# Two rounds of attention at a time, an earlier start of the weight fold, and copies that walk in the order of their target

## The chip, the cores and the metric

One core of a Trainium2 chip runs the whole program. The metric is the time of one execution on the device, in microseconds (us). The core's engines run side by side, each through a queue of its own in a fixed order: TensorE (PE, with its weight loads PEld), VectorE (DVE), ScalarE (ACT), GpSimd (POOL), and SyncE (SP), which here only issues DMA transfers. Matmul results land in PSUM, which is cut into banks of 512 float32 per partition; everything else on the chip lives in SBUF.

## The reference

Windowed attention over 4 batches, 8 heads, 576 positions and 64 dimensions; heads 0 to 3 see the last 32 positions ("plain"), heads 4 to 7 see 32 positions with a step of 4 ("dilated"). Two MLPs follow, over 2304 tokens.

```python
scores = scale * np.matmul(q, k.transpose(0, 1, 3, 2))
attn = softmax(np.where(mask, scores, -1e9))      # mask_plain or mask_dil, by head
x = np.matmul(attn, v).transpose(0, 2, 1, 3).reshape(B * S, H * D)   # 2304 x 512
h = x @ w_in ; x = np.maximum(0.01 * h, h) @ w_out                   # 512 -> 2048 -> 512
a = x @ w1 ; b = x @ w2 ; out = ((a * b) @ w3) @ w_out2              # 512 -> 1024 -> 1024 -> 512
```

The weights of the MLPs are float64 in memory. The kernel keeps float32 precision by splitting both operands of a product into a high and a low part and adding three matmuls.

## The kernel before

**MLP 1** runs over seven chunks of tokens, `c` = 0 to 6: 320 and 256 tokens of batch 0 (c 0, 1), the same of batch 1 (c 2, 3), then three chunks of 384 tokens that cover batches 2 and 3. In a chunk, 16 turns `f` of 128 hidden units each: `hidden_steps` makes 12 matmuls into one of two PSUM banks (`ps_h`, `bank`, L95), ACT takes the result out as `g` (L563), DVE and POOL split it into `gs` (L110, L112), and two turns later `project_steps` makes 12 matmuls into `ps_x`. A new `ps_h` has to wait until ACT has taken out the one two turns earlier.

**Attention** is cut into 32 rounds: a pair of heads and 5 or 4 blocks of 64 queries (r = 0 or 1). Rounds 0 to 15 (batches 0, 1) lie in an order written out by hand (`START`, under `manual_schedule`), which also holds the first MLP turns. Rounds 16 to 31 (batches 2, 3) come from the generator `attention` (L511), of which `pace` (L949) advances so many steps in each MLP turn. One round is: `scores` (64-row matmuls into `ps_s`, L394; mask, maximum and exponentials on DVE and ACT), `normalize` (DVE, POOL), `turn_p` (transposes `ps_p`, L451; copies to `pT` on ACT), `value_steps` (64-column matmuls `ps_o`, L472; ACT and DVE write the high and low part of x, L500 and L503). `ps_s`, `ps_p` and `ps_o` share the two banks of `side_bank` (L92). q and k come by `load_qk`, and are turned by PE and copied out of PSUM (`turn_rows`, L374) for batches 0 and 1, turned by DVE (`turn_halves`) for 2 and 3.

**The fold** computes w3 @ w_out2 on the chip, during the chunks c = 4 and 5. It converts 24 float64 blocks (`Convert`: fetch by DMA as `rawf`; POOL and ACT scale, ACT makes two halves as `rf`, DVE joins them as `wf`), splits them (`keep_wo2`, `keep_w3`: ACT and DVE or POOL), stores the 8 blocks of w_out2 to memory and loads them again four times (`load_wo2`), and multiplies (`wp_step`). It begins at `LATE`, turn (4, 13), in `begin_fold`, which first lets attention run out and closes its SBUF pool `att`; the pool `fold` takes that space. `FOLD_PACE` makes 1.35 steps of it in each turn. In the last chunk, c = 6, w1 and w2 are converted in the same way and the product is loaded again and split (`load_wp` into `wpf`, `split_wp` into `wps`, `raww`, `wr` and `w` for the weights). **MLP 2** follows with `gate` (`ps_ab`) and `final` (`ps_y`).

Outside `START` the order on each queue is made at build time by a planner: of what is ready by its own model of durations it takes what stands first in the program. The chip then follows this order on each engine, whatever the real durations are.

Of the kernel before, what the change touches and what calls it, by code (L numbers as in the profile page):

```python
# [8 lines left out]
F32 = mybir.dt.float32  # L9
# [13 lines left out]
DILATION = 4  # L23
# [5 lines left out]
def tile_window_attention_two_mlps(  # L29
# [224 lines left out]
    def load_halves(m, src, o):  # L254


        pi, nm = seq[m // 2], "qk"[m % 2]
        t = att.tile([P, NT, D], F32, tag="nat", name=f"{nm}{pi}", bufs=2)
        for g in range(P // E):
            og = o + g // 2 * S * D + g % 2 * E  # L260
            to = t[g * E : (g + 1) * E]
            x = NT * D - E
            nc.sync.dma_start(
                to.rearrange("p n d -> p (n d)")[:, :x], rows(src, og, [[NT * D, E], [1, x]])
            )
        nat_t[nm, pi] = t

    def turn_halves(m):
        pi, nm = seq[m // 2], "qk"[m % 2]
        t = nat_t.pop((nm, pi))  # L270
        dst = att.tile([P, S], F32, tag=nm + "T", name=f"{nm}T{pi}", bufs=2)
# [85 lines left out]
    def turn_rows(m):  # L357
        pi, nm = seq[m // 2], "qk"[m % 2]
        plain = pair(pi)[2]
        c = 6 if plain else 8  # L360
        n = S // c
        t = nat_t.pop((nm, pi))
        ps = bank2(f"ps_{nm}T{pi}")
        for g in range(2):
            for c1 in range(c // 2):
                src = t[:n, g * (c // 2) + c1].rearrange("p j d -> p (j d)")
                nc.tensor.transpose(ps[:, g, c1 * n : (c1 + 1) * n], src, ident[:n, :n])
        yield
        dst = att.tile([P, S], F32, tag=nm + "T", name=f"{nm}T{pi}", bufs=2)
# [89 lines left out]
    def value_steps(n):  # L459
# [24 lines left out]
        else:  # L484
            spans = []
            for g in range(DILATION):
                j0, j1 = max(0, s0 - g * SR), min(SR, s1 - g * SR)
                if spans and spans[-1][2:] == (j0, j1):
                    spans[-1] = (spans[-1][0], spans[-1][1] + 1, j0, j1)
                elif j0 < j1:  # L490
                    spans.append((g, 1, j0, j1))
# [19 lines left out]
    def attention(n0, n1):  # L511
# [7 lines left out]
        scores(n0)  # L519
        yield  # L520
        scores(n0 + 1)
        normalize(n0)
        yield
        for n in range(n0, n1):
# [12 lines left out]
            run(value_steps(n))  # L537
            m = n // NA * 4
            if n % NA in (2, 3):
                load_v(m + n % NA)  # L540
            elif n % NA in (5, 7):
                load_v(m + 4 + (n % NA == 7))
# [122 lines left out]
    def keep_w3(i):  # L665


        def finish(w, e_hi, e_lo):
# [7 lines left out]
            t = fold.tile([P, 2, 2, NG * P], F32R, tag="w3T", name=f"w3T{i}", bufs=2)  # L676
            split(t[:, 0], t[:, 1], ps.rearrange("p (j r) -> p j r", j=2), e_hi, nc.vector)
            w3T.extend((i // (NI // NG), i % (NI // NG) * 2 + j, t[:, :, j]) for j in range(2))
# [28 lines left out]
    def load_wp(ib):  # L707
        t = late.tile([P, DM], F32, tag="wpf", name=f"wpf{ib}", bufs=1)
# [58 lines left out]
    with ExitStack():  # L767
        make_identity(nc, ident)
        att_es, att = pool("att", "right")
        mask_d = masks = att.tile([P, S // QB, KB], BF16, name="masks")  # L770
        nc.vector.memset(masks, 0.0)
        def build_masks():
# [32 lines left out]
            "K": (rawp, "kr", 2), "W": (woB_p, "woB", NF // 2), "N": (att, "nat", 2), "V": (att, "v", 2)  # L805
# [105 lines left out]
        LATE = (4, 13)  # L911
        FOLD_PACE = 1.35
# [18 lines left out]

        def begin_fold():
            step(*[stream] * 200)
            att_es.close()
            nonlocal fold, fold_es, conv3
            fold_es, fold = pool("fold", "right")
            jobs = [(load_rows, w_out2, jb, keep_wo2(jb)) for jb in range(NI)]
            jobs += [(load_w3, w3, i, keep_w3(i)) for i in range(NI * NI // NG // 2)]

            def fold_tile(tag, dt, bufs):  # L940
                return lambda i: fold.tile([P, 512], dt, tag=tag, name=f"{tag}f{i}", bufs=bufs)

            conv3 = Convert(
                jobs, fold_tile("raw", U64, 2), fold_tile("w", I32, 2), fold_tile("r", I32, 2),
                FOLD_CONV,
            )
            conv3.fetch(2)

        def pace(c):  # L949

            owed[0] += 39 / 28 if c < LATE[0] else 2.25
# [7 lines left out]
        for c, f0, f1 in runs:  # L959
# [4 lines left out]
            if c == NCH - 1:  # L964
                while conv3.made < len(conv3.jobs) or conv3.done or w3T:
                    fold_step()
                fold_es.close()
                first_es, first_y = pool("first", "right")
# [97 lines left out]
```

## Time and profile before

| | us |
|---|---|
| median of 3 runs | 869.25 (868.57 to 869.71) |
| the profiled execution | 868.56 |
| its span, from the first to the last instruction | 866.6 |
| PE busy / PEld busy | 848.2 / 772.0 |
| DVE, ACT, POOL busy | 346.7, 352.6, 210.8 |
| attention of batches 2 and 3 and the MLP turns beside it | about 198 to 362 |
| the fold | about 362 to 495 |
| last chunk of MLP 1 with the conversion of w1 and w2 | about 500 to 568 |

Times in the rows are counted from the first instruction. An engine's busy time is the union of its instructions; matmuls overlap, so the distance between their starts tells PE's pace, and a duration does not. A row's bracket gives the idle time before it and what ended that time. The granted clock is TensorE's, as a share of 2.4 GHz.

### The profile page before, as it was taken

The numbers are of one execution on the slowest core, as the hardware profiler recorded it, in microseconds if no ns is written. First come the engines' busy times: TensorE is split into PE (matmuls) and PEld (weight loads), VectorE is DVE, ScalarE is ACT, GpSimd is POOL, SyncE is SP. The second block draws the span as 40 slices with busy tenths as digits, with TensorE's granted clock in tenths as the row PEclk, the third lists the DMA queues.
The fourth block names the chain that finished last, engine by engine and source line by source line (L and its number), as shares of the span: only waits on it lengthen the run. The fifth ranks groups of instructions, "written<-read, shape, count | busy, mean of one in ns | idle before, by whom it ended". The sixth has DMA issues, their size and how long they took to land.

```text
span 866.6 us, 14693 instructions
## 1 busy us (share of the span) xinstructions
PE 848.2 (98%) x5774; PEld 772.0 (89%) x5774; DVE 346.7 (40%) x704; ACT 352.6 (41%) x879; POOL 210.8 (24%) x236
## 2 busy tenths in 40 slices
PE   7999998999999999999999999999999999999998
PEld 7799997999999999989899999998888888888887
DVE  4999976344453432274434177731021011000000
ACT  4999945223443343364433175632131121111111
POOL 3311101122322232263222134223123112111110
PEclk9999999999999999999999999999999999999999
DMA  6976575183333311189887575341001000000001
GB/s 152 309 214 231 179 169 137 34 193 73 82 98 92 78 45 50 47 294 349 300 289 236 165 239 155 113 135 49 25 1 61 24 13 13 25 12 13 25 13 48
DMA packets 87333, 103.58 MB, mean 120 GB/s; under 512 B 42849, under 2 KB 65633, under 8 KB 87265
## 3 DMA queue, kind: packets, MB, share of 16 engines
q1 hardware_dynamic: 87264, 102.65, 39.0%
q8 instruction: 45, 0.74, 0.4%
q14 instruction: 24, 0.19, 0.1%
HBM read 85.72 MB, written 16.91 MB: 118 GB/s over the span
## 4 chain that ended last, share of the span: by engine, by line
PE 77%; DMA 7%; DVE 6%; ACT 5%; issue 4%; POOL 2%; SPq 0%; POOLq 0%; DVEq 0%; ACTq 0%
PE ps_ab L120 7%; PE ps_ab L122 7%; PE ps_ab L121 7%; PE ps_x L120 6%; PE ps_x L122 5%; PE ps_x L121 5%; PE ps_h L120 5%; PE ps_h L122 5%; PE ps_h L121 5%; PE ps_y L122 4%; PE ps_y L121 4%; PE ps_y L120 4%; PE ps_s L394 2%; PE ps_o L472 2%; PE ps_wp L122 2%
## 5 line engine op out<-in xcount | busy, mean ns | idle before, releaser
L120 PE MATMUL ps_h<-x,win 128*128 128x384 f32 (+2 forms) x448 | 142.5, 318 | 4.9 <-ACT g L563 4.2
L122 PE MATMUL ps_h<-x,win 128*128 128x384 f32 (+2 forms) x448 | 140.7, 314 | 0.0
L121 PE MATMUL ps_h<-x,win 128*128 128x384 f32 (+2 forms) x448 | 140.4, 313 | 0.0
L120 PE MATMUL ps_x<-gs,wout 128*128 128x384 f32 (+2 forms) x368 | 119.0, 325 | 0.0
L743 DVE TENSOR_TENSOR ab<-a,ps_ab 128x512 f32<-128x512 f32 (+1 forms) x40 | 25.2, 633 | 233.3 <-ACT a L741 225.8
L120 PE MATMUL ps_ab<-ys,w 128*128 128x512 f32 (+1 forms) x320 | 117.7, 368 | 0.6 <-DVE ab L743 0.6
L121 PE MATMUL ps_x<-gs,wout 128*128 128x384 f32 (+2 forms) x368 | 117.7, 320 | 0.1
L122 PE MATMUL ps_ab<-ys,w 128*128 128x512 f32 (+1 forms) x320 | 117.7, 368 | 0.0
L121 PE MATMUL ps_ab<-ys,w 128*128 128x512 f32 (+1 forms) x320 | 117.6, 368 | 0.0
L122 PE MATMUL ps_x<-gs,wout 128*128 128x384 f32 (+2 forms) x368 | 117.4, 319 | 0.0
L112 POOL TENSOR_TENSOR p<-ab,p 128x512 fp32r<-128x512 f32 (+1 forms) x40 | 47.0, 1177 | 211.3 <-ACT p L110 211.3
L110 DVE CAST gs<-g 128x384 fp32r<-128x384 f32 (+2 forms) x92 | 41.3, 449 | 128.9 <-ACT g L563 103.3
L120 PEld LDWEIGHTS ps_h<-x,win 128*128 128x128 f32 x448 | 84.8, 189 | 8.2 <-ACT g L563 6.1
L112 POOL TENSOR_TENSOR gs<-g,gs 128x384 fp32r<-128x384 f32 (+2 forms) x64 | 59.5, 929 | 133.5 <-DVE gs L110 133.5
L563 ACT ACTIVATE g<-ps_h 128x384 f32<-128x384 f32 (+2 forms) x112 | 49.1, 439 | 96.8 <-PE ps_h L122 80.2
L121 PEld LDWEIGHTS ps_h<-x,win 128*128 128x128 f32 x448 | 84.9, 190 | 0.3
L122 PEld LDWEIGHTS ps_h<-x,win 128*128 128x128 f32 x448 | 84.8, 189 | 0.4
L741 ACT COPY a<-ps_ab 128x512 f32<-128x512 f32 (+1 forms) x40 | 21.6, 543 | 139.5 <-PE ps_ab L122 139.5
L120 PEld LDWEIGHTS ps_x<-gs,wout 128*128 128x128 f32 x368 | 69.5, 189 | 1.7
L121 PEld LDWEIGHTS ps_x<-gs,wout 128*128 128x128 f32 x368 | 69.7, 189 | 1.3 <-POOL gs L112 0.4
L122 PEld LDWEIGHTS ps_x<-gs,wout 128*128 128x128 f32 x368 | 69.7, 189 | 0.6
L120 PEld LDWEIGHTS ps_ab<-ys,w 128*128 128x128 f32 x320 | 60.1, 188 | 11.1 <-DVE ab L743 1.0
(109 smaller groups left out, 1553.1 us busy)
## 6 DMA issues: line engine op xcount, KB each, us to landing
wo<-wo_dram SPq DMA_DIRECT2D x32, 512.0 KB
raw<-in_moe_w_in_dram SPq DMA_DIRECT2D x16, 512.0 KB
raw<-in_moe_w_out_dram SPq DMA_DIRECT2D x16, 512.0 KB
rawf<-in_moe_w_dram SPq DMA_DIRECT2D x16, 512.0 KB
raww<-in_moe_w_dram SPq DMA_DIRECT2D x16, 512.0 KB
q<-in_q_dram SPq DMA_DIRECT2D x48, 140.0 KB
k<-in_k_dram SPq DMA_DIRECT2D x48, 140.0 KB
v<-in_v_dram SPq DMA_DIRECT2D x60, 96.0 KB
```

The costliest lines, as they stand in the source:

```text
L110: copy_on(e_hi)(hi, src)
L112: e_lo.tensor_tensor(lo, src, hi.bitcast(F32), op=ALU.subtract)
L120: nc.tensor.matmul(ps, a[1], b[0], start=first, stop=False)
L121: nc.tensor.matmul(ps, a[0], b[1], start=False, stop=False)
L122: nc.tensor.matmul(ps, a[0], b[0], start=False, stop=last)
L394: nc.tensor.matmul(ps[j * QB : (j + 1) * QB, i - bl.start], qt[d, i * QB : (i + 1) * QB], kt[d, first_key(i, plain) : first_key(i, plain) ...
L472: nc.tensor.matmul(ps[j * D : (j + 1) * D, i * QB : (i + 1) * QB], vt[i][:, h + j, :], t[:, i, j * QB : (j + 1) * QB], start=True, stop=True,)
L563: nc.scalar.activation(g, ps, AF.Prelu, alpha=SLOPE)
L741: nc.scalar.copy(t, ps[0][:, :n])
L743: nc.vector.tensor_tensor(g, t, ps[1][:, :n], op=ALU.mult)
```

## The change

It does five things.

1. **Two rounds at a time**: `attention` steps through rounds n and n + 1 together, in four steps instead of eight: transposes of n; transposes of n + 1 with the turning and loading of q and k; values of both; scores and normalization of the next two. `pace` takes 22/28 and 14/13 steps a turn instead of 39/28 and 2.25. Where the next batch begins (n % 8 == 4), turning and loading come after the scores.
2. **An own pool for q and k**: `nat`, `qT` and `kT` move from `att` to a new pool `qkp`, which stays open until the last chunk.
3. **Earlier fold**: at turn (4, 10) `begin_conv` makes the fold's `Convert` with its buffers in the slots of `nat`, `qT` and `kT`, and fetches two blocks; at (4, 13) one conversion step comes ahead of `begin_fold`.
4. **Buffers**: the transposed blocks of w3 are kept as two halves with 3 buffers, instead of whole with 2, and are split half by half; `wpf` has 2 buffers instead of 1.
5. **Order of copies**: the copies of q and k out of PSUM and the dilated copies of x go through their elements in the order in which these lie in the target.

```diff
-        t = att.tile([P, NT, D], F32, tag="nat", name=f"{nm}{pi}", bufs=2)
+        t = qkp.tile([P, NT, D], F32, tag="nat", name=f"{nm}{pi}", bufs=2)
...
         if plain:
-            to = dst.rearrange("d (p g c) -> d g c p", g=2, p=n)
+            to, dims = dst.rearrange("d (p g c) -> d p g c", g=2, p=n), "d g (c p) -> d p g c"
         else:
-            to = dst.rearrange("d (c p g) -> d g c p", g=2, p=n)
-        copy_on(engine_of[TURN_ON[m]])(to, ps[:, :, : S // 2].rearrange("d g (c p) -> d g c p", p=n))
+            to, dims = dst.rearrange("d (c p g) -> d c p g", g=2, p=n), "d g (c p) -> d c p g"
+        copy_on(engine_of[TURN_ON[m]])(to, ps[:, :, : S // 2].rearrange(dims, p=n))
...
-            x = x.rearrange("d i (j r) -> d i r j", r=DILATION)
-            for g, m, j0, j1 in spans:
+            x = x.rearrange("d i (j r) -> d i j r", r=DILATION)
+            edges = sorted({0, s0 % SR, s1 % SR, SR})
+            for j0, j1 in zip(edges, edges[1:]):
+                g = [g for g in range(DILATION) if s0 <= g * SR + j0 and g * SR + j1 <= s1]
                 src = bass.AP(
-                    ps.tensor, ps.offset + g * SR + j0 - s0,
-                    [list(ps.ap[0]), [SR, m], [1, j1 - j0]],
+                    ps.tensor, ps.offset + g[0] * SR + j0 - s0,
+                    [list(ps.ap[0]), [1, j1 - j0], [SR, len(g)]],
                 )
-                views.append((x[:, :, g : g + m, j0:j1], src))
+                views.append((x[:, :, j0:j1, g[0] : g[-1] + 1], src))
...
+        for n in range(n0, n1, 2):
             run(turn_p(n))
-            normalize(n + 1)
             yield
-            if n % 8 != 3:
-                scores(n + 2)
-                yield
-            transpose_qk(n + 4)
-            load_qk(n + 6)
+            run(turn_p(n + 1))
+            turn = [lambda m=m: (transpose_qk(m), load_qk(m + 2)) for m in (n + 4, n + 5)]
+            if n % NA != 4:
+                for f in turn:
+                    f()
             yield
-            if n % 8 == 3:
-                scores(n + 2)
-                yield
-            run(value_steps(n))
+            for i in (n, n + 1):
+                run(value_steps(i))
...
+            yield
+            for i in (n + 2, n + 3):
+                scores(i)
+            if n % NA == 4:
+                for f in turn:
+                    f()
+            for i in (n + 2, n + 3):
+                normalize(i)
             yield
...
-            t = fold.tile([P, 2, 2, NG * P], F32R, tag="w3T", name=f"w3T{i}", bufs=2)
-            split(t[:, 0], t[:, 1], ps.rearrange("p (j r) -> p j r", j=2), e_hi, nc.vector)
+            for j in range(2):
+                t = fold.tile([P, 2, NG * P], F32R, tag="w3T", name=f"w3T{i}_{j}", bufs=3)
+                split(t[:, 0], t[:, 1], ps[:, j * NG * P : (j + 1) * NG * P], e_hi, nc.vector)
...
-        t = late.tile([P, DM], F32, tag="wpf", name=f"wpf{ib}", bufs=1)
+        t = late.tile([P, DM], F32, tag="wpf", name=f"wpf{ib}", bufs=2)
...
+        CONV_AT = (4, 10)
...
+        def begin_conv():
+            nonlocal conv3
+            jobs = [(load_rows, w_out2, jb, keep_wo2(jb)) for jb in range(NI)]
+            jobs += [(load_w3, w3, i, keep_w3(i)) for i in range(NI * NI // NG // 2)]
+
+            def words(tag, dt):
+                return lambda i: qkp.tile([P, 512], dt, tag=tag, name=f"{tag}f{i}", bufs=2)
+
+            conv3 = Convert(jobs, words("nat", U64), words("qT", I32), words("kT", I32), FOLD_CONV)
+            conv3.fetch(2)
...
-            owed[0] += 39 / 28 if c < LATE[0] else 2.25
+            owed[0] += 22 / 28 if c < LATE[0] else 14 / 13
...
+                if (c, f) == CONV_AT:
+                    begin_conv()
                 if (c, f) == LATE:
+                    conv3.step()
                     begin_fold()
```

## Rows read from the trace of the kernel before

**Rows 1.** The page's first part: busy time, share of the span, instructions.

```profile
PE 848.2 (98%) x5774; PEld 772.0 (89%) x5774; DVE 346.7 (40%) x704; ACT 352.6 (41%) x879; POOL 210.8 (24%) x236
```

**Rows 2.** Stretches: length, busy PE, PEld, DVE, ACT, POOL, clock, DMA share, GB/s.

```profile
345.00:361.80 16.80, 16.80 (x122) 15.81 (x121) 1.93 (x5) 3.49 (x9) 3.05 (x3) 1.00 0.01 3
...
385.40:388.70 3.30, 3.30 (x12) 3.30 (x11) 3.16 (x4) 1.56 (x3) 2.76 (x3) 0.50 0.98 315
388.80:400.00 11.20, 11.07 (x66) 10.69 (x65) 4.38 (x8) 6.62 (x11) 5.50 (x6) 1.00 1.00 369
198.00:362.00 164.00, 164.00 (x1522) 154.62 (x1521) 61.61 (x155) 62.88 (x241) 45.28 (x52) 1.00 0.28 69
```

**Rows 3.** PE in order of time: start, duration; two rounds' values at once.

```profile
156.50 0.28 PE L121 MATMUL ps_x<-gs,wout 128*128 128x256 f32 x1
156.62 0.28 PE L122 MATMUL ps_x<-gs,wout 128*128 128x256 f32 x1
156.83 1.39 PE L472 MATMUL ps_o<-pT,v 96*64 96x64 f32 x40
...
158.37 0.28 PE L121 MATMUL ps_x<-gs,wout 128*128 128x256 f32 x1
```

**Rows 4.** PE in order of time: one round's values.

```profile
269.67 0.28 PE L122 MATMUL ps_h<-x,win 128*128 128x256 f32 x1
269.88 0.69 PE L472 MATMUL ps_o<-pT,v 96*64 96x64 f32 x16
...
270.71 0.28 PE L121 MATMUL ps_x<-gs,wout 128*128 128x256 f32 x1
```

**Rows 5.** PE in order of time: two rounds' scores at once.

```profile
177.50 0.31 PE L122 MATMUL ps_x<-gs,wout 128*128 128x320 f32 x1
177.74 1.54 PE L394 MATMUL ps_s<-kT,qT 64*64 64x96 f32 x32
...
179.46 0.31 PE L121 MATMUL ps_x<-gs,wout 128*128 128x320 f32 x1
```

**Rows 6.** PE in order of time: one round's scores.

```profile
246.42 0.28 PE L121 MATMUL ps_h<-x,win 128*128 128x256 f32 x1
246.63 0.88 PE L394 MATMUL ps_s<-kT,qT 64*64 64x96 f32 x16
...
247.66 0.28 PE L120 MATMUL ps_x<-gs,wout 128*128 128x256 f32 x1
```

**Rows 7.** PE: the first and the last of the small-matmul runs between 198 and 362.

```profile
198.43 0.34 PE L472 MATMUL ps_o<-pT,v 96*64 96x64 f32 x4
...
359.31 0.34 PE L472 MATMUL ps_o<-pT,v 96*64 96x64 f32 x4
```

**Rows 8.** PE and ACT in order of time, where the fold begins.

```profile
381.70 0.34 PE L121 MATMUL ps_h<-x,win 128*128 128x384 f32 x1
381.87 0.34 PE L122 MATMUL ps_h<-x,win 128*128 128x384 f32 x1
384.26 0.45 PE L120 MATMUL ps_h<-x,win 128*128 128x384 f32 x1 [2.05 <-ACT g L563]
...
361.89 0.78 ACT L151 ACTIVATE rf<-rawf 128x512 f16<-128x512 f32 x1
...
381.96 0.62 ACT L110 CAST wo<-wf 128x512 fp32r<-128x512 f32 x1 [2.70 <-DVE wf L157]
```

**Rows 9.** PE and ACT in order of time, in the last chunk of MLP 1.

```profile
545.86 0.44 PE L120 MATMUL ps_h<-x,win 128*128 128x384 f32 x1 [0.65 <-ACT g L563]
...
544.80 0.62 ACT L110 CAST wps<-wpf 128x512 fp32r<-128x512 f32 x1 [0.24 <-DMA wpf<-wp_dram]
```

**Rows 10.** Copies out of PSUM: minimum, median, maximum ns; by shape: busy, mean ns.

```profile
L374 DVE COPY kT<-ps_kT x3: 760/1184/1202, 8.9 to 25.8; 128x576 f32<-128x576 f32 x3
...
L500 ACT CAST x<-ps_o 128x288 fp32r<-128x288 f32 x8 | 5.4, 676 | 9.2 <-PE ps_o L472 9.2
...
L500 ACT CAST x<-ps_o 128x320 fp32r<-128x320 f32 x8 | 3.4, 419 | 2.0 <-PE ps_o L472 2.0
```

More of the change, by code (lines that the diff above doesn't have):

```diff
@@ L270, in turn_halves @@
         t = nat_t.pop((nm, pi))
-        dst = att.tile([P, S], F32, tag=nm + "T", name=f"{nm}T{pi}", bufs=2)
+        dst = qkp.tile([P, S], F32, tag=nm + "T", name=f"{nm}T{pi}", bufs=2)
         if pair(pi)[2]:
@@ L368, in turn_rows @@
         yield
[L369 removed]
+        dst = qkp.tile([P, S], F32, tag=nm + "T", name=f"{nm}T{pi}", bufs=2)
         if plain:
[L371 removed]
+            to, dims = dst.rearrange("d (p g c) -> d p g c", g=2, p=n), "d g (c p) -> d p g c"
         else:
[L373 to L374 removed]
+            to, dims = dst.rearrange("d (c p g) -> d c p g", g=2, p=n), "d g (c p) -> d c p g"
+        copy_on(engine_of[TURN_ON[m]])(to, ps[:, :, : S // 2].rearrange(dims, p=n))
         qk_t[nm, pi] = dst
@@ L518, in attention @@
         load_v(n0 // 2 + 1)
-        scores(n0)
+        for n in (n0, n0 + 1):
+            scores(n)
         yield
-        scores(n0 + 1)
-        normalize(n0)
+        for n in (n0, n0 + 1):
+            normalize(n)
         yield
-        for n in range(n0, n1):
+        for n in range(n0, n1, 2):
             run(turn_p(n))
-            normalize(n + 1)
             yield
-            if n % 8 != 3:
-                scores(n + 2)
-                yield
-            transpose_qk(n + 4)
-            load_qk(n + 6)
+            run(turn_p(n + 1))
[3 more added lines that the diff above has]
+                    f()
             yield
-            if n % 8 == 3:
-                scores(n + 2)
-                yield
-            run(value_steps(n))
+            for i in (n, n + 1):
+                run(value_steps(i))
             m = n // NA * 4
[L539 to L542, printed above, removed]
+            if n % NA == 2:
+                load_v(m + 2)
+                load_v(m + 3)
+            elif n % NA in (4, 6):
+                load_v(m + 2 + n % NA // 2)
+            yield
[6 more added lines that the diff above has]
+                normalize(i)
             yield
@@ L675, in finish @@
                     )
-            t = fold.tile([P, 2, 2, NG * P], F32R, tag="w3T", name=f"w3T{i}", bufs=2)
-            split(t[:, 0], t[:, 1], ps.rearrange("p (j r) -> p j r", j=2), e_hi, nc.vector)
-            w3T.extend((i // (NI // NG), i % (NI // NG) * 2 + j, t[:, :, j]) for j in range(2))
+            for j in range(2):
+                t = fold.tile([P, 2, NG * P], F32R, tag="w3T", name=f"w3T{i}_{j}", bufs=3)
+                split(t[:, 0], t[:, 1], ps[:, j * NG * P : (j + 1) * NG * P], e_hi, nc.vector)
+                w3T.append((i // (NI // NG), i % (NI // NG) * 2 + j, t))
         return finish
@@ L768, in tile_window_attention_two_mlps @@
         make_identity(nc, ident)
+        qkp_es, qkp = pool("qk", "right")
         att_es, att = pool("att", "right")
@@ L804, in tile_window_attention_two_mlps @@
         homes = {
-            "K": (rawp, "kr", 2), "W": (woB_p, "woB", NF // 2), "N": (att, "nat", 2), "V": (att, "v", 2)
+            "K": (rawp, "kr", 2), "W": (woB_p, "woB", NF // 2), "N": (qkp, "nat", 2), "V": (att, "v", 2)
         }
@@ L934, in begin_fold @@
             att_es.close()
-            nonlocal fold, fold_es, conv3
+            nonlocal fold, fold_es
             fold_es, fold = pool("fold", "right")
[L937 to L947, printed above, removed]
         def pace(c):
-            owed[0] += 39 / 28 if c < LATE[0] else 2.25
+            owed[0] += 22 / 28 if c < LATE[0] else 14 / 13
             while owed[0] >= 1:
@@ L967, in tile_window_attention_two_mlps @@
                 fold_es.close()
+                qkp_es.close()
                 first_es, first_y = pool("first", "right")
```

7 lines of the change are left out of this document (removed).

## The prediction

> **What bounds the kernel now.** I read the page first, for which engine is full; then PE's waits and a table of stretches, for where PE is not; then the timeline of each place found. PE is busy 848.2 of 866.6 us, no other engine half the span [rows 1], so a microsecond is only worth something if PE's own stream gets shorter or one of PE's waits goes. From 198 to 362 us, beside the attention that this change regroups, PE is never idle: 164.00 of 164.00 busy, while DVE, ACT and POOL stand at 62, 63 and 45 [rows 2]. Nothing is to be won there by hiding work, only by making PE's stream cheaper. Behind that, PE stands still in two places that the change touches: 2.05 us at 382, where the fold starts [rows 8], and three waits in the last chunk of MLP 1, of which the longest is 0.65 us [rows 9]. Ahead of 160 us the order is by hand, and PE waits in many places for the copies of q, k and x.
>
> **The sum is made against the profiled execution**, 868.56 us, of which 866.6 are the span; the median of the runs is 869.25, so 0.69 us are added at the end.
>
> **Pairs of rounds.** The reader is to compare runs of small matmuls (scores, values) that stand between the large ones. The price of a run is the distance from the start of the last large matmul before it to the start of the second one behind it, less two ordinary distances (0.12 us at 256 columns, by the first two of [rows 3]; in proportion 0.15 at 320). One round's values, 16 instructions: 270.71 - 269.67 - 0.24 = 0.80 us [rows 4]. Two rounds' values at once, 40 instructions: 158.37 - 156.62 - 0.24 = 1.51 us [rows 3]. So 24 more instructions cost 0.71 us, 0.030 each, and a run costs 0.80 - 16 x 0.030 = 0.33 us before its first instruction counts. Scores: one round 247.66 - 246.42 - 0.24 = 1.00 us [rows 6], two rounds of the same size 179.46 - 177.50 - 0.30 = 1.66 us [rows 5]; the second costs 0.66, and joining saves 0.34. The switch between small and large matmuls costs a third of a microsecond, and the hand-written part already shows both joined forms.
>
> Between 198.43 and 359.31 [rows 7] I count 30 such runs: 16 rounds' scores and 16 rounds' values, one of the latter cut in two, with three places where scores and values touch. In pairs there are 8 and 8, so 14 switches go, 14 x 0.33 = 4.6 us. The transposes of P (`ps_p`) are in PE's full-size form and I give them nothing. Against the full 4.6 speaks that the order is the planner's: both banks of `side_bank` must be free at once, and a pair is cut if the second bank comes late. The steps lie 28/22 = 1.3 turns apart, some 4 us or more, and what empties the banks (two copies of 0.4 to 0.7 us on ACT, then DVE) fits into that. I take 11 of the 14, **-3.6 us**; bounds -4.6 and 0. The bursts (nine exponentials instead of four or five) are no new work, and ACT is idle 100 of these 164 us [rows 2]; were that cover gone, `g` would be late and PE wait as at 384 [rows 8]. A load of q, k or v moves by at most one round on SP's queue, where nothing is queued from memory that PE needs in that turn.
>
> **The fold's first blocks.** At 381.87 PE issues its last `ps_h` matmul and at 384.26 the next, 2.39 us instead of 0.17: 2.2 us lost. The cause is in ACT's fixed order: `g`, which frees the bank, is queued behind the split of a converted block (`wo`), and that waited 2.70 us for DVE's join [rows 8]. Right behind, from 385.40 to 388.70, the granted clock is 0.50, the 1.2 GHz level, though PE is busy throughout [rows 2]: half of 3.30, 1.65 us, is lost. I read it as the stall's consequence, since the clock is 1.00 in the stretches before and after. Together 3.9 us.
>
> The conversions are late because they begin late and then in a burst: the first starts at 361.89 [rows 8], when attention's pool is closed, and the memory queues go from 3 GB/s (345 to 361.8) to a share of 1.00 at 369 GB/s (388.8 on) [rows 2]. The change gives the first blocks buffers that are free once the last scores have read q and k, and one step more at turn (4, 13): the stream is ahead by at least one step, 1/1.35 of a turn. A turn is 24 matmuls at 0.17 us (the first two of [rows 8]), 4.1 us, so the lead is 3.0 us, more than the 2.05 us of the wait. What hides the added step is an empty stretch: from 345 to 361.8 ACT works 3.5 of 16.8 us, DVE 1.9, POOL 3.1 [rows 2]. The two fetches stand behind no load that attention still needs; without that cover, a block is 0.5 MB, and at 369 GB/s that is 1.4 us each. What is late next is the memory stream itself. I take **-3.3 us**, with bounds -3.9 and 0. The two half splits of w3 add 16 small instructions each to ACT and DVE; beside a loaded PE they cost nothing unless they delay `g` (rival 3).
>
> **The second buffer of `wpf`.** In the last chunk ACT waits 0.24 us for the loaded block ahead of its split, and `g` behind it holds PE for 0.65 us [rows 9]. There are three such waits of PE in a row, 0.33, 0.65 and 0.28 us, 1.26 in all. A second buffer takes the wait for the load away; it does not shorten the rest of that loop. **-0.6 us**, bounds -1.3 and 0.
>
> **Order of the copies.** DVE copies the same 576 elements of k in 760 ns for the dilated pair, whose neighbours lie 8 bytes apart in the target, and in 1184 to 1202 for plain ones, 24 bytes apart; ACT's dilated x (16 bytes apart) takes 676 ns for 288 elements against 419 for 320 in a row [rows 10]. So a scattered target costs. In target order four copies of q and k gain up to 0.43 us, and a dilated round some 0.3 us on ACT and 0.2 on DVE, all of it off PE. In the hand-written part PE waits for DVE and ACT in places, so some comes through: **-0.5 us**, from -2 to, if reading PSUM by steps is itself slow, +1.7 (below). No row shows such a read.
>
> The Trainium skill, SBUF — State Buffer, section Door 1: The DMA port swizzle, says that SBUF is served in lines of 16 bytes, full speed needing at least two accesses to a line, and agrees with [rows 10]. It says in the same place that PSUM's lines are 8 bytes and that any non-contiguous PSUM pattern significantly slows matmuls; it does not speak of copies. That speaks against this part of the change, and no run shown here tests it; it is rival 4.
>
> **Sum**: -3.6 - 3.3 - 0.6 - 0.5 = -8.0; 868.56 - 8.0 + 0.69 = **861.2 us**.
>
> **Rivals.** (1) The fold's stall stays or moves a turn: memory is full from 388.8 on [rows 2], ACT still waits in order for it, and the planner's durations don't know that. For it: the first block is converted the moment the pool is free [rows 8], so its fetch was early already. Against: one step of lead is 3.0 us. 861.2 + 3.3 = 864.5. (2) The pairs don't form: the planner puts large matmuls between the two rounds for want of a bank. For it: one round was cut in two, and its second piece stands in [rows 7]. 861.2 + 3.6 = 864.8. Both (1) and (2): 868.1, no change. (3) Slower: three half buffers for w3 where two whole ones held four halves. When a block's second half is split, the first half of the block before must have been multiplied, so ACT and DVE wait for PE's own `wp_step`, with `g` queued behind them. One such hold is priced like the one at 384: 2.2 + 1.65 = 3.9 us. Two eat the gain (868.9); from the third in 16 blocks on it is slower: 861.2 + 11.6 = 872.8. Against: the planner sees this dependence and orders around it. (4) Reading PSUM by steps is as slow as the scattered write was: plain copies stay at 1.18, four dilated ones rise by 0.42, 1.7 us on the head's chain at most. 861.2 + 0.5 + 1.7 = 863.4.
>
> **How the numbers follow.** A measurement of this kernel tells about 0.2% from no change, 1.7 us. Forecast 0.43 (861.2), rival 1 0.17, rival 2 0.12, rival 4 0.08, all of them faster: 0.80. Both 1 and 2: 0.08, within. Rival 3: 0.12, slower. The low end takes every term near its bound, -4.6 - 3.9 - 1.3 - 2 = -11.8, which is 857.5; the high end, 868.0, leaves out the last two cases, 0.20.
>
> **What would show it.** Pairs: runs of 32 to 40 scores and of 32 to 40 values between 198 and 360, some 16 to 19 runs, PE still full. Fold: ACT's first `rf` well before 361.89 less what was gained, no wait of PE over 1 us between 360 and 400, and the clock 1.00 there; a wait for `g` with the clock at 0.50 behind it says rival 1. Last chunk: ACT's wait for `wpf` gone and PE's three waits below 0.7 us in sum. Copies: L374 at about 0.76 us for all; at 1.1 or more, rival 4. ACT or DVE waiting for `ps_wp` ahead of w3T: rival 3. I am wrong altogether if PE shows new waits between 198 and 360, where it has none.

## The result, and the profile after

| | before | after |
|---|---|---|
| median of 4 runs, us | 868.91 (867.23 to 869.71) | 876.47 (873.91 to 876.99) |
| profiled execution / its span, us | 868.56 / 866.6 | 875.96 / 874.2 |
| ratio after to before | | 1.0084, 95% interval 1.0058 to 1.0109 |

The forecast was 861.2 us. The change makes the kernel slower by 0.84%, and the range (857.5 to 868.0) doesn't hold the time. In all that follows, a ratio is turned into microseconds with 868.5 us for the kernel before, whose medians beside the experiments were 867.3 to 868.5.

The page's first part of the kernel after, to be set against [rows 1]:

```profile
PE 847.7 (97%) x5774; PEld 775.9 (89%) x5774; DVE 339.7 (39%) x720; ACT 350.5 (40%) x895; POOL 208.2 (24%) x236
```

PE is busy as long as before, in a span that is 7.6 us longer. So the new time stands where PE is idle or slow. Stretches of the kernel after (columns as in [rows 2]), and a last row with the stretch 380 to 400 of the kernel before:

```profile
345.00:361.80 16.80, 16.80 (x154) 16.06 (x153) 7.41 (x17) 10.29 (x29) 5.95 (x8) 1.00 0.19 65
361.80:372.20 10.40, 10.40 (x88) 10.03 (x87) 1.60 (x5) 3.66 (x10) 2.47 (x3) 1.00 0.00 0
380.00:400.00 20.00, 8.39 (x30) 7.59 (x30) 8.46 (x12) 9.53 (x15) 8.66 (x9) 0.70 0.91 318
386.30:391.40 5.10, 5.07 (x16) 5.08 (x17) 2.22 (x5) 1.94 (x3) 1.98 (x3) 0.51 0.96 303
398.50:401.70 3.20, 3.14 (x12) 3.15 (x13) 0.43 (x2) 1.37 (x3) 0.66 (x1) 0.53 1.00 388
```

```profile
380.00:400.00 20.00, 17.82 (x94) 17.11 (x93) 11.73 (x18) 11.56 (x20) 11.36 (x12) 0.91 0.93 333
```

Between 380 and 400 us PE works 8.39 us where it worked 17.82. Behind each of the long waits the granted clock is at half, the 1.2 GHz level (0.51 for 5.10 us, 0.53 for 3.20). And from 361.8 to 372.2 the memory is silent (0 GB/s), in the stretch where the kernel before had already begun to convert (first `rf` at 361.89 [rows 8]). PE's waits from 370 to 470 us, by what they waited for (us in total, times, longest):

```profile
PE ps_w3T L674 <- DVE qTf L157: 6.6, 1, 6.6
PE ps_x L121 <- POOL gs L112: 3.1, 1, 3.1
PE ps_x L120 <- ACT st L636: 1.9, 1, 1.9
PE ps_w3T L674 <- ACT g L565: 0.7, 1, 0.7
PE ps_wp L120 <- ACT st L695: 0.6, 1, 0.6
PE ps_w3T L674 <- DVE w3T L112: 0.3, 1, 0.3
PE ps_wp L120 <- DVE w3T L112: 0.2, 1, 0.2
```

These are 13.4 us in sum, against the one wait of 2.05 in this stretch before [rows 8]. The longest in order of time, PE from 391.45 on:

```profile
391.45 0.34 PE L121 MATMUL ps_x<-gs,wout 128*128 128x384 f32 x1
391.63 0.34 PE L122 MATMUL ps_x<-gs,wout 128*128 128x384 f32 x1
398.56 1.12 PE L674 MATMUL ps_w3T<-ident,qTf 128*128 128x128 f32 x4 [6.59 <-DVE qTf L157]
399.32 0.67 PE L120 MATMUL ps_h<-x,win 128*128 128x384 f32 x1
```

PE stands before the first four transposes of w3 and waits for DVE's join of that block. The hidden matmuls of turn (5, 3) stand right behind them in PE's order; ACT had taken out the `ps_h` ahead of them, and with it freed their bank, by 378.6. The Trainium skill, PSUM — Partial Sum Buffer, section Engine vs sequencer instructions, says that matmuls start and complete in program order; this row agrees, 6.59 us of it.

What was forecast of the pairs is there. PE in order of time, the values and the scores of two rounds:

```profile
257.82 0.28 PE L121 MATMUL ps_h<-x,win 128*128 128x256 f32 x1
257.94 0.28 PE L122 MATMUL ps_h<-x,win 128*128 128x256 f32 x1
258.15 1.39 PE L472 MATMUL ps_o<-pT,v 96*64 96x64 f32 x40
...
259.69 0.28 PE L121 MATMUL ps_x<-gs,wout 128*128 128x256 f32 x1
...
262.17 1.54 PE L394 MATMUL ps_s<-kT,qT 64*64 64x96 f32 x32
```

Between 198 and 370 there are 7 runs of 32 to 40 scores and 8 of 32 to 40 values; only the scores of the first pair stand apart, at 198.8 and 202.6. If every run of attention's matmuls from 198 to 380 is priced as in the forecast (transposes of P with them), their sum falls from 39.4 us in 52 runs to 34.4 in 33. At turn (5, 2) PE is 4.3 us ahead of the kernel before (375.67 against 379.97). Yet attention itself ends later. All values, scores and transposes of P after 325 us in the kernel after (ns minimum, median, maximum; first and last start):

```profile
L394 PE MATMUL ps_s<-kT,qT x72: 242/243/294, 327.7 to 351.9; 64*64 64x96 f32 x72
L451 PE MATMUL ps_p<-ident,s x18: 271/273/273, 337.0 to 365.9; 128*96 128x128 f32 x18
L472 PE MATMUL ps_o<-pT,v x72: 221/222/271, 345.6 to 370.9; 96*64 96x64 f32 x72
```

The last value matmul starts at 370.9 and not at 359.4 [rows 7]. The fold's pool opens behind it, so the first split of a converted block starts at 371.44 (ACT; 365.88 before), although the first conversion started 10.4 us earlier. ACT in order of time, in that stretch:

```profile
351.48 0.79 ACT L151 ACTIVATE kTf<-natf 128x512 f16<-128x512 f32 x1 [1.83 <-PE ps_s L394]
...
353.41 0.78 ACT L153 ACTIVATE kTf<-natf 128x512 int16<-128x512 uint32 x1
354.05 0.35 ACT L418 ACTIVATE s<-s,nmax 128x96 f32<-128x96 f32 x1
...
359.70 0.76 ACT L153 ACTIVATE kTf<-natf 128x512 int16<-128x512 uint32 x1
...
370.71 0.84 ACT L495 CAST x<-ps_o 128x256 fp32r<-128x256 f32 x2 [1.81 <-PE ps_o L472]
371.44 1.14 ACT L110 CAST wo<-qTf 128x512 fp32r<-128x512 f32 x2
```

The early conversions, the first two of the four instruction pairs ahead of the last pair's exponentials, are done by 360.5. Then they stop: the two slots of `qTf` hold the first two converted blocks until the splits have a pool to write to.

The other two parts, copies out of PSUM and the last chunk. DVE's copies of q and k in the kernel after:

```profile
L374 DVE COPY qT<-ps_qT x3: 748/749/758, 6.6 to 23.3; 128x576 f32<-128x576 f32 x3
L374 DVE COPY kT<-ps_kT x3: 743/758/758, 8.9 to 25.3; 128x576 f32<-128x576 f32 x3
```

All take what the dilated ones took (760 [rows 10]). In the last chunk PE's three waits for `g` [rows 9] are gone, and the distance to the kernel before falls from 9.9 us at turn (6, 10) to 7.6 at the end.

**The account** of the 7.6 us between the spans: waits from 370 to 470, 13.4; half clock behind them, 5.10 x 0.49 + 3.20 x 0.47 = 4.0; less the same place before, 3.9 (the forecast's 2.2 + 1.65); pairs -5.0; last chunk -2.3. Sum +6.2; the other 1.4 I can't put down to one place.

### The profile page after: what moved, and what is told of

Read it like the earlier page. It is cut to its first block, busy times and chain, and to the rows that moved or that the text cites. A ratio compares the mean times of both kernels' runs of the same rounds, so it can differ in the third digit from the quotient of the medians.

```text
span 874.2 us, 14743 instructions
## 1 busy us (share of the span) xinstructions
PE 847.7 (97%) x5774; PEld 775.9 (89%) x5774; DVE 339.7 (39%) x720; ACT 350.5 (40%) x895; POOL 208.2 (24%) x236
## 4 chain that ended last, share of the span: by engine, by line
PE 48%; DMA 3%; issue 2%; ACT 1%; POOL 1%; DVE 0%; SPq 0%; ACTq 0%; POOLq 0%
PE ps_ab L120 7%; PE ps_ab L121 7%; PE ps_ab L122 7%; PE ps_y L121 4%; PE ps_y L120 4%; PE ps_y L122 4%; PE ps_x L120 2%; PE ps_x L121 2%; PE ps_x L122 2%; PE ps_h L121 2%; PE ps_h L122 2%; PE ps_h L120 2%; PE ps_wp L120 1%; PE ps_wp L122 1%; PE ps_wp L121 1%
## 5 line engine op out<-in xcount | busy, mean ns | idle before, releaser
L110 DVE CAST gs<-g 128x384 fp32r<-128x384 f32 (+2 forms) x92 | 33.4, 363 | 130.6 <-ACT g L565 107.9
```

Of the source, the lines that this page charges most:

```text
L110: copy_on(e_hi)(hi, src)
```

## The experiments

Theory A: pairs in this order make attention end late, while PE's fixed order still has the fold's first products at an early turn, so PE runs into blocks that are not yet converted. Theory B: the fold's early blocks are at fault. Theory C: the ring of three halves for w3 is (rival 3 of the forecast). Kernels differ from the kernel after in the parts named; ratios are to the kernel before, run on the same chip. In the diffs, which are cut to the lines that matter ("..."), "-" is the kernel after, unless said otherwise.

### Parts alone

Pairs only: the fold begins as before.

```diff
-                if (c, f) == CONV_AT:
-                    begin_conv()
                 if (c, f) == LATE:
-                    conv3.step()
                     begin_fold()      # fetches the first two blocks itself, into its own pool
...
-                t = fold.tile([P, 2, NG * P], F32R, tag="w3T", name=f"w3T{i}_{j}", bufs=3)
+            t = fold.tile([P, 2, 2, NG * P], F32R, tag="w3T", name=f"w3T{i}", bufs=2)
```

> The changed kernel with the fold begun as before (its own pool, first fetch when attention's pool closes, whole w3T tiles, two of them); pairs, order of copies and second wpf buffer stay. Theory A (pairs of rounds form a serial chain of about 23 us a pair, attention's last values land at 370 us where they landed at 359, and the fold, which waits for them, runs into PE's fixed order): nearly as slow as the changed kernel, 872 to 877 us, last ps_o run between 366 and 371 us, PE waits over 2 us between 370 and 410. Theory B (the early blocks of the fold are at fault: their conversions stand ahead of the last softmax and the planner sets w3T's transposes too early): 863 to 867, since the cheaper attention is then kept. Theory C (ring of three half w3T tiles): also 863 to 867.

Early fold only: `attention` and `pace` as in the kernel before, the rest as after.

```diff
-            owed[0] += 22 / 28 if c < LATE[0] else 14 / 13
+            owed[0] += 39 / 28 if c < LATE[0] else 2.25
```

> The changed kernel with attention in single rounds as before; early fold, half w3T tiles, order of copies and second wpf buffer stay. Theory A (late attention): its last values land near 359 to 361 us again, the stall at the fold's start is gone or small, 864 to 867 us. Theory B (early blocks): slower, 872 us or more, with PE waiting 3 us or more ahead of w3T's transposes. Theory C (ring of three halves): slower too, with ACT or DVE waiting for wp_step's matmuls before they write w3T.

Neither: both diffs together, so that only copies and `wpf` are left of the change, and the pool `qkp`, which all kernels here have but `wpf` only.

> Single rounds and the fold as before; of the change only the order of the copies and the second wpf buffer stay. All theories: the stall of 2 us at 382 stays, PE's three waits in the last chunk (1.26 us) go. By the trace of the changed kernel the last chunk gains 2.2 us and the head nothing: 868.9 - 2.2 = 866.7, within 865.5 to 868. If the copies alone are what loses, 872 or more.

Then the second `wpf` buffer alone and the copies alone, each put into the kernel before:

```diff
-        t = late.tile([P, DM], F32, tag="wpf", name=f"wpf{ib}", bufs=1)
+        t = late.tile([P, DM], F32, tag="wpf", name=f"wpf{ib}", bufs=2)
```

> The kernel before with a second wpf buffer and nothing else. By the trace of the kernel with single rounds and the fold as before (864.9 us, 3.3 below the kernel before), all that it gains shows behind 380 us and the order of the copies gains nothing by 160 us: so this one should reach 865 to 867. If the order of the copies has a part in it: 867.5 to 868.5.

```diff
-            to = dst.rearrange("d (p g c) -> d g c p", g=2, p=n)
+            to, dims = dst.rearrange("d (p g c) -> d p g c", g=2, p=n), "d g (c p) -> d p g c"
...
-            x = x.rearrange("d i (j r) -> d i r j", r=DILATION)
+            x = x.rearrange("d i (j r) -> d i j r", r=DILATION)
```

> The kernel before with the copies of q, k and x in the order of their target and nothing else. DVE's plain copies of q and k fall from about 1.19 to 0.75 us, and ACT's 96-wide dilated ones from 0.68 to under 0.4; none of it is PE's. The forecast was -0.5 us; the difference of the runs with and without the copies, both with the second wpf buffer, says 0 within 1 us: 868 to 869 here.

| kernel | us | ratio, 95% interval |
|---|---|---|
| copies only | 867.97 | 1.0010 (0.9997 to 1.0023) |
| `wpf` only | 865.60 | 0.9964 (0.9951 to 0.9976) |
| copies and `wpf` ("neither") | 864.88 | 0.9970 (0.9956 to 0.9984) |
| the same and pairs | 873.09 | 1.0066 (1.0041 to 1.0092) |
| the same and the early fold with the ring of halves | 869.43 | 1.0014 (0.9998 to 1.0031) |
| all (the change) | 876.47 | 1.0084 (1.0058 to 1.0109) |

Pairs alone cost 0.0096, 8.3 us. The early fold with its ring costs 3.8 us without pairs and 1.6 with them (there the intervals overlap). So theory A has the larger part, and B or C a smaller one. `wpf` gains 3.1 us (2.1 to 4.3) and the copies nothing. The prices of B and C in the expectations were wrong: nearly as slow with pairs alone is what A said, but the early fold alone is neither below 867, as A said, nor above 872, as B did; and "neither" came out 0.6 us below its range. What `wpf` gains shows in PE's waits from 530 to 590, first the kernel before, then `wpf` only:

```profile
PE ps_h L120 <- ACT g L563: 1.2, 3, 0.6
PE ps_ab L120 <- DVE ab L743: 0.6, 1, 0.6
```

```profile
PE ps_ab L120 <- DVE ab L743: 0.6, 1, 0.6
```

PE's only wait between 355 and 470 us with pairs alone:

```profile
PE ps_w3T L674 <- DVE wf L157: 12.2, 1, 12.2
```

and its stretch from 389 to 401, in which PE does nothing:

```profile
389.00:401.00 12.00, 0.00 (x0) 0.00 (x0) 5.66 (x11) 6.51 (x10) 4.81 (x5) 0.69 0.87 278
```

One wait, larger than the whole loss. The instructions of the traces, counted by turns, say where it stands:

```
                               last values     first w3 transposes    time from the one
                               behind turn     behind turn, start     to the other
before                         (4, 13)  359.4    (5, 4)  395.0          35.6 us, no wait
pairs only                     (5, 0)   368.7    (5, 3)  401.1          32.4 us, wait 12.2
the change                     (5, 0)   370.9    (5, 2)  398.6          27.7 us, wait 6.6
```

From the last values to the first block of w3, eight blocks of w_out2 and this one must be converted and split (in the change two of them are converted ahead of it); 26 to 36 us lie between the two in the kernels here. Before, PE had seven turns to do meanwhile. With pairs it has three or two, and then it stands still.

### The scores ahead of the values

If A holds, it is enough that attention ends on time. In the kernel before, the scores of the next but one round stood before the values of the present one; in the change they stand behind. Put back, for pairs:

```diff
+            for i in (n + 2, n + 3):
+                scores(i)
...
+            yield
             for i in (n, n + 1):
                 run(value_steps(i))
...
-            yield
-            for i in (n + 2, n + 3):
-                scores(i)
...
             for i in (n + 2, n + 3):
                 normalize(i)
```

> The changed kernel with one step moved: the scores of the next pair stand before the values of the present one (before: behind them), so that the softmax of the next pair runs beside this pair's last copy of P and its values. Theory A: the chain of a pair gets shorter by 4 to 9 of its 23 us, the last values land before 362 us, the wait at the fold's start shrinks below 2 us, and the time falls to 862 to 867. Theories B and C: the time stays at 873 to 877, since the early fold and the ring are unchanged.

The same with the fold as before (the diff of pairs only on top), and with the fold as before but the ring of halves (that diff without its last two lines):

> Pairs with the scores of the next pair ahead of this pair's values, the fold begun as before with two whole w3T tiles; order of copies and second wpf buffer stay. Theory A (only the late end of attention made pairs dear): the last values land near 356 us, the fold starts as with single rounds, and the pairs' cheaper small matmuls (39.4 us of PE for runs of small matmuls between 198 and 380 without pairs, 34.4 with) come through: 864.9 - 3 to 5 = 860 to 862 us. Rival D (PE's fixed order takes whatever attention gains and waits for the fold's conversions, since these are bound by memory from 362 us on): 864 to 867, with a wait of 3 us or more ahead of w3T's transposes.

> Pairs with scores ahead of values, the fold begun as before, w3T in half tiles in a ring of three. With the run before it in this set and the kernel with the early fold (863.5 us) it divides ring and early fold where attention is not late. Theory C: the ring costs 3 to 5 us against whole tiles, and the early fold gives something back. Theory B: ring and whole tiles are equal within 1 us, and the early fold costs.

| scores ahead of values, and | us | ratio, 95% interval |
|---|---|---|
| all the rest of the change | 863.50 | 0.9949 (0.9934 to 0.9964) |
| fold as before | 860.18 | 0.9907 (0.9893 to 0.9922) |
| fold as before, ring of three halves | 858.68 | 0.9892 (0.9878 to 0.9907) |

One step in another place turns +7.3 us into -4.4. In the kernel with the fold as before, the values after 325 us and PE's waits from 345 to 470:

```profile
L472 PE MATMUL ps_o<-pT,v x72: 222/222/270, 335.7 to 355.7; 96*64 96x64 f32 x72
```

```profile
PE ps_x L120 <- DVE gs L110: 1.4, 1, 1.4
PE ps_x L121 <- POOL gs L112: 0.6, 1, 0.6
```

Attention ends at 355.7 and the wait for w3's transposes is gone. The pairs are now worth 0.9907 - 0.9970, -5.5 us: what PE saved all the time and lost again. Rival D, that PE's order would eat this gain, falls.

### The place of the fold

The other way round: attention stays as late as it is, and the fold stands three turns later in the program, with 1.45 steps a turn for 1.35. First with pairs only, then in the change itself with all its parts:

```diff
-        LATE = (4, 13)
-        FOLD_PACE = 1.35
+        LATE = (5, 0)
+        FOLD_PACE = 1.45
...
-            owed[0] += 22 / 28 if c < LATE[0] else 14 / 13
+            owed[0] += 22 / 28 if c < 4 else 14 / 13
```

> Pairs with attention as late as in the change, fold with whole w3T tiles, but the fold's place in the program three turns later, (5, 0) instead of (4, 13), with 1.45 steps a turn instead of 1.35, so that PE's order has w3T's first transposes behind turn (5, 6) instead of (5, 3). If the wait of 12 us is only a matter of place in PE's order (the first converted block comes 31 us after attention's pool is closed, whenever that is): the wait shrinks below 3 us and the time falls to 861 to 866. If the memory stream is what loses (the fold then ends late and holds up the last chunk): the waits move behind 460 us and the time stays above 868.

> The changed kernel itself, all its parts kept, with the fold's place in the program moved from turn (4, 13) to (5, 0) and 1.45 steps a turn for 1.35; PE's order then has w3T's first transposes behind turn (5, 6) instead of (5, 2). If late attention against a fixed place of the fold is the cause of the loss: the waits of 6.6, 3.1 and 1.9 us between 383 and 399 go, and the time falls by 11 to 15 us, to 861 to 866. If ring or shared slots lose by themselves: 868 or more.

Measured: 861.83 us, ratio 0.9938 (0.9916 to 0.9960), and 861.77 us, 0.9925 (0.9904 to 0.9946). The change with its fold three turns later is 13.8 us faster than the change (0.0159), and reaches the time that was forecast. Its stretch from 380 to 400 and its waits from 345 to 470:

```profile
380.00:400.00 20.00, 19.31 (x112) 18.43 (x110) 11.81 (x16) 11.53 (x20) 13.57 (x14) 1.00 0.93 306
```

```profile
PE ps_wp L120 <- DMA wo<-wo_dram: 0.5, 1, 0.5
PE ps_x L120 <- ACT st L636: 0.5, 1, 0.5
```

The last values still land at 370 us, and the memory moves no more per second (306 GB/s) than in the slow kernel (318). PE merely has other turns to do meanwhile. The waits, not the lateness by itself and not the memory, were the loss.

### What made attention late: the written pace or the chain

One number changed on top of pairs only:

```diff
-            owed[0] += 22 / 28 if c < LATE[0] else 14 / 13
+            owed[0] += 28 / 28 if c < LATE[0] else 14 / 13
```

> Pairs in the order of the change (next scores behind this pair's values), fold begun as before, whole w3T tiles, and one number changed: attention takes 28 of its steps in 28 turns where it took 22, as the single rounds took 39 of twice as many steps. Theory A1 (the written pace made attention late: four steps a pair at 22/28 a turn are 5.1 turns a pair): the last values land near 332 us, the wait of 12 us ahead of w3T's transposes goes, and the time is 859 to 863 us. Theory A2 (the chain of a pair, scores to softmax to P to values, is what takes 22 us, whatever the pace): PE waits for P or for the exponentials between 200 and 345 us, where it had no wait so far, the last values land no earlier than 350, and the time is 866 or more.

In this kernel some values land in `x` before MLP turns that stand behind them have read the rows of the batch before, so part of the MLP's input is other than the reference's; the instructions are the same ones. 870.3 us, 1.0039 (1.0017 to 1.0061). Theory A1 missed. Of A2 the time came and PE's waits came, the place didn't quite: the last values start at 348.2 to 349.1, neither near 332 nor after 350. PE has a hole where there was none, 9.0 us between 262 and 300. There the steps of a pair stand back to back, with no MLP turn between them:

```profile
275.12 1.70 PE L394 MATMUL ps_s<-kT,qT 64*64 64x96 f32 x36 [0.83 <-DVE x L498]
282.77 1.30 PE L451 MATMUL ps_p<-ident,s 128*96 128x128 f32 x5 [5.95 <-POOL s L435]
...
285.98 2.19 PE L472 MATMUL ps_o<-pT,v 96*64 96x64 f32 x36 [0.41 <-ACT pT L455]
288.60 0.74 PE L394 MATMUL ps_s<-kT,qT 64*64 64x96 f32 x6 [0.43 <-DVE x L498]
```

So the bare chain of a pair, from scores to the next scores, takes 13.5 us here (the clock is 0.82 from 262 to 300), 7.65 of them from the scores to the first transpose. In the change the pace gives this part, the softmax, one step: 28/22 = 1.3 turns ahead of chunk 4, but 13/14 of a turn, 3.9 us, in it. Where a step stands in the program follows from `pace`; where PE has it is counted by turns in the traces:

```
                                                in the program    on PE behind
scores of a pair, the change                       (3, 13)           (3, 14)
scores of the next pair                            (4, 1)            (4, 3)
scores of the next pair                            (4, 5)            (4, 8)
scores of the last pair                            (4, 9)            (4, 12)
last values, the change                            (4, 12)           (5, 0)
last values, before                                (4, 12)           (4, 13)
last values, scores ahead, fold as before          (4, 13)           (4, 13)
last values, 28 steps in 28 turns                  (4, 6)            (4, 9)
```

The written pace ends attention at the same turn before and after the change, so it isn't what made it late. The change is one turn behind its program up to chunk 4 and loses three more in it: a pair has 3.7 turns there by the pace and takes four to five. With the scores ahead of the values the softmax has two steps, and no turn is lost; a quicker pace ahead of chunk 4 moves the end, and a lag of three turns stays. So it is the chain, by its order of steps; that the softmax is the part of it that doesn't fit is read from 7.65 against 3.9 us, and no run changes the softmax alone. That the clump of steps comes from reads of `x` is argued, not shown; by its time alone the run decides nothing between pace and chain.

### The smaller part: ring and early step

The fold begins as before in the next four, and w3 is kept in halves: with single rounds and a ring of three, with single rounds and a ring of four, with the pairs of the change and a ring of three, and with scores ahead of values and a ring of four.

```diff
-                if (c, f) == CONV_AT:
-                    begin_conv()
                 if (c, f) == LATE:
-                    conv3.step()
                     begin_fold()
...
-                t = fold.tile([P, 2, NG * P], F32R, tag="w3T", name=f"w3T{i}_{j}", bufs=3)
+                t = fold.tile([P, 2, NG * P], F32R, tag="w3T", name=f"w3T{i}_{j}", bufs=4)
```

> Single rounds, the fold begun as before, but w3T split into half tiles in a ring of three; order of copies and second wpf buffer stay. It divides the loss of the early fold (869.4 against 864.9 us without it). If the ring is the cause (theory C): 868 to 870 with PE waits between 400 and 470 us. If the early conversions and the sharing of their slots are (theory B): 864 to 866.

> Single rounds, fold begun as before, w3T in half tiles in a ring of four, which is the memory of two whole tiles; with a ring of three it took 870.0 us, with whole tiles 864.9. If the short ring costs: 864 to 866. If the halves cost (16 more small splits on ACT and DVE, another order), whatever the ring: 869 to 871.

> The change without the early blocks: pairs, half ring of three, fold begun as before; it divides the 3.4 us between pairs with whole tiles (873.1) and the changed kernel (876.5). PE's order has w3T's transposes behind turn (5, 3), as with whole tiles, and in the changed kernel behind (5, 2). If that place makes the difference: 872 to 874, with one wait near 12 us. If the ring does: 875 to 878.

> Pairs with scores ahead of values, fold begun as before, half tiles in a ring of four: with a ring of three 858.7 us, with whole tiles 860.2. If a longer ring helps: 857 to 858.5, the lowest so far. If the ring never binds where attention is on time: 858 to 860.

| w3 as | single rounds | pairs as in the change | pairs, scores ahead |
|---|---|---|---|
| two whole tiles | 0.9970 | 1.0066 | 0.9907 |
| halves, ring of three | 1.0016 (1.0005 to 1.0027) | 1.0060 (1.0037 to 1.0084) | 0.9892 |
| halves, ring of four | 0.9978 (0.9965 to 0.9990) | not run | 0.9910 (0.9886 to 0.9934) |

In microseconds the four new ones are 869.96, 873.65 and, for the ring of four, 866.22 and 860.35. The pairs of the change with the ring of three wait 11.8 us ahead of w3's transposes, as expected if the place in PE's order makes the difference. The ring of three costs 4.0 us with single rounds, and a fourth half takes 3.3 of them back; so its length is what costs there. PE's waits from 395 to 500 sum to 4.8 us with three, 1.9 with four and 0.6 with whole tiles. One hold of the ring, ACT with single rounds and three halves, waiting for PE's products:

```profile
479.38 0.37 ACT L110 CAST w3T<-ps_w3T 128x256 fp32r<-128x256 f32 x1 [3.28 <-PE ps_wp L122]
```

With pairs, in either order, the ring costs nothing that can be measured, though such holds are there (ACT waits 3.1 us in three of them in the change). Theory C is a true mechanism, and not the cause here.

That leaves the early blocks. Scores ahead of values, all the rest of the change, without the one step at (4, 13):

```diff
                 if (c, f) == LATE:
-                    conv3.step()
                     begin_fold()
```

> Pairs with scores ahead of values, half ring, the fold's first blocks in the q and k slots as in the change, but without the added conversion step at turn (4, 13). With step it took 863.5 us, without the early slots at all 858.7. If the added step costs (it moves w3T's transposes and products nearer to their data in PE's order): 858 to 860, waits ahead of w3T behind 440 us gone. If the slots cost (two raw slots shared with q and k, fetches at turn (4, 10)): 862 to 865.

858.99 us, 0.9902 (0.9881 to 0.9924). The added step costs 0.0047, 4.1 us: with it PE's order has the first transposes of w3 behind (5, 2), without it behind (5, 3). The early slots by themselves are worth nothing (0.9902 against 0.9892 without them). Slots and step together cost 5.0 us here (0.9949 against 0.9892), 2.1 in the change itself (1.0084 against 1.0060, intervals that overlap), and nothing with single rounds (1.0014 against 1.0016).

## Why the prediction was wrong, step by step

**Pairs, -3.6.** The price of a switch held, and 15 of the 16 runs were joined; the term was too small, -5.0 in PE's time and -5.5 us in the kernel where it comes through. But the forecast costed only PE's stream and took attention's end as given. It asked of the order of steps for the banks alone ("the steps lie 28/22 = 1.3 turns apart") and not for the softmax, which with the scores of a pair behind the values of the one before stands in one such step with nothing to overlap: 7.65 us, against 3.9 in chunk 4. So attention's last values start at 370.9 and not at 359.4, behind turn (5, 0) and not (4, 13). "Ahead by at least one step" was said of the fold and not asked of attention, which the fold waits for. This is the step that failed. What the runs showed in its place: attention late against a PE order that has the fold's first products behind turn (5, 2), which gives 13.4 us of waits from 370 to 470 and some 4.0 us of half clock, and both go when either side is moved.

**Fold start, -3.3.** It gained in no kernel, and cost up to 5.0 us. The lead was real (first conversion 10.4 us earlier) and idle: two slots, and splits that wait for a pool, the first of them 5.6 us later than before. The price of "one step more" had the wrong sign: a conversion that stands a step earlier in the program moves its products earlier in PE's order, whatever the memory does (4.1 us with the scores ahead). Rival 1 had the reason in words (the planner's durations don't know the memory) and let it cost only the gain. Nor was the 1.65 us of half clock in this term a fixed cost: the kernel with `wpf` only has the same order on PE up to 480 us, waits 1.4, 0.7 and 0.7 us at the fold's start, and its clock from 384 to 392 is 1.00.

**Second `wpf` buffer, -0.6.** Measured -3.1 (2.1 to 4.3), beyond the bound of -1.3. The halving of the three waits was wrong, since all three went (`wpf` only has no wait of PE over 0.1 us there), and idle time is not the whole price: in the kernel before, PE's starts around the three waits, less the ordinary 0.17, lose 2.06 us where the waits sum to 1.26. The third of them, where 0.62 us lie between two starts and 0.28 of that is idle:

```profile
549.95 0.34 PE L122 MATMUL ps_x<-gs,wout 128*128 128x384 f32 x1
550.57 0.45 PE L120 MATMUL ps_h<-x,win 128*128 128x384 f32 x1 [0.28 <-ACT g L563]
```

With the second buffer 0.33 of the 2.06 is left. The 1.7 us so gained lie below the interval of the 3.1; no trace shows what the rest is (the two profiled executions differ by 2.1 us, 868.56 and 866.44).

**Copies, -0.5.** The mechanism held (0.75 us for all copies on DVE), the gain didn't come through: +0.9 us (-0.3 to 2.0). Rival 4 falls: a copy that reads PSUM by steps is as quick as one that reads in a row. The sentence of the Trainium skill, SBUF — State Buffer, section Door 1: The DMA port swizzle, on non-contiguous PSUM patterns does not carry over from matmuls to these copies.

**Rivals.** Slower was given 0.12, as rival 3 at 872.8. The side came true and the time is near by luck, by another mechanism; the holds that it named are there in the change, and cost time only with single rounds (4.0 us). Rival 2 came true for one run of 16, the first pair's scores.

**Tell-tales.** "New waits between 198 and 360" was the wrong place to look for being wrong: PE is full there in the change too. It looks full because the late work is waited for 20 to 40 us further on.

## What to carry to other kernels

Before a step of an interleaved stream is regrouped, set what lies between two of its steps (here a softmax of 7.65 us) against the time that the pace leaves for it (3.9 us), count the turns by which it ends late, and ask which later stage opens at its end and how many turns PE's fixed order leaves that stage for its first data. What the busy engine saves is only kept if whatever is timed against it moves along: here 5 us saved cost 12 until three turns were put in between. An early start on an engine that isn't the bound gains nothing when its output has nowhere to go, and its place in the program pulls the consumers forward.

## What the runs showed of the hardware

A wait of PE costs more than its idle time: three waits of 1.26 us in sum lost 2.06 us by the starts around them. Where PE stood still for 1.4 and 0.6 us (pairs with scores ahead, fold as before) the granted clock from 372 to 400 stayed 1.00; behind waits of 3.1 and 1.9 us in the change it was 0.51 for 5.1 us, and behind 6.6 us 0.53 for 3.2 us. Length alone doesn't tell: 2.05 us before was followed by 0.50 [rows 2, 8], 2.1 us with single rounds and the ring of three by 1.00 from 385 to 440, and 1.4, 0.7 and 0.7 us at the fold's start with `wpf` only by 1.00 from 384 to 392. DVE needs 743 to 758 ns for 576 elements read from PSUM by steps and written in a row, 1184 to 1202 the other way round [rows 10]; so for these copies it is the side in SBUF that counts.
